# Mixing the first batch over its keys, scores two pairs ahead, and pooling by accumulating DMAs in a fused attention and MLP kernel

## The chip, the cores and the metric

The kernel runs on one core of one Trainium2 chip. A core has TensorE (PE, with its weight loads shown as PEld), VectorE (DVE), ScalarE (ACT), GpSimd (POOL) and SyncE (SP), each with its own queue of instructions that is worked through in order, and 16 DMA engines. The metric is the device time of one execution in microseconds (us), as the median of several executions. The profile is of one execution by the hardware profiler.

## The reference

Three stages follow one another. B = 8 batches, H = 8 heads, S = 576 positions, D = 64, so 512 channels.

```python
k_p = k.reshape(B, H, Sp, pool, D).mean(axis=3)      # pool = 8, Sp = 72 keys
v_p = v.reshape(B, H, Sp, pool, D).mean(axis=3)
attn = softmax(q @ k_p^T / 8)                        # rows over the 72 keys
x = attn @ v_p                                       # heads joined: B x 576 x 512
h = x^T @ U @ V                                      # mixing over positions, rank 32
u = x + h^T
x = u + relu(u @ w_ch1) @ w_ch2                      # first MLP, 512 -> 2048 -> 512
xn = layernorm(x) * g_ln
out = x + relu(xn @ w_ch1') @ w_ch2'                 # second MLP
```

`U` (576 x 32), `V` (32 x 576) and the weights arrive as 64-bit floats, and the kernel turns them into 32-bit ones itself.

## The kernel before, in words

Two heads make a pair, so a batch has four pairs and the kernel has 32 (the first pair has the number P = 0). For each pair the kernel loads q, k and v (`att_load`), adds the eight neighbours of each key and value (`att_prep`, `att_prep_v`: one reduction or a tree of additions, on DVE or POOL), makes five tiles of scores on PE (`att_s`), finds the extreme of each row and takes exponentials and the normalization (`att_m`: DVE, ACT, then DVE or POOL), turns the result so that keys lie on partitions (`att_t`), and multiplies by the values (`att_av`), which leaves x of the pair as `xT`. When the four pairs of a batch are done, x is turned back tile by tile (`att_xt`), split into a high and a low part, multiplied by U (`att_g`, `att_gs`) and by V (`att_vm`), and DVE adds the product to `xT`. That is u. The first MLP works on groups of 512 positions: `a_l1` makes a hidden block of 128 channels from four `hid` pairs (high and low part of u) and the weights `wh` and `wl`, `a_l2` multiplies it on. Eight hidden blocks stay resident, and the rest is done in later passes whose weights are decoded and stored meanwhile.

Every weight block must be decoded first: 64-bit words are loaded into `wraw` or `araw`, and five DVE instructions (the first may be ACT's) and a split into `wh` and `wl` follow. This goes on beside the attention.

Nothing is issued in the order in which it is written. Each operation is recorded with its possible engines, an assumed cost on each, and a priority: the sum of PE cost recorded before it, plus a bias. A list scheduler (`Order.schedule`) then gives every operation an engine and a place, and the buffers of a ring are handed out in the order of the program. What the program writes earlier therefore has priority, but an assumed cost decides the place. The instructions of an engine then run in that fixed order, whatever the real times are. Before, all DMAs but one small load are issued by SP.

In the steps of a batch, pair P's turning and multiplying are interleaved with the scores of pair P + 1:

```python
S_ = [s(N, t) for t in range(5)] if N < B * NP else [None] * 5   # N = P + 1
seq = [S_[0], R_[2], S_[1], T_[0], S_[2], S_[3], T_[1], S_[4], T_[2], R_[1], M_, V_[0]]
```

## Time and profile before

| | |
|---|---|
| median of 3 runs | 1776.09 us (1772.47 to 1776.58) |
| the profiled execution, its own time | 1774.35 us |
| its span (first to last instruction) | 1772.6 us |
| PE busy in the span | 1738.5 us (98%) |
| DVE, ACT, POOL busy | 973.2, 723.8, 745.9 us (55%, 41%, 42%) |

The profiled execution lies 1.7 us under the median, and 1.75 us of its time lie outside the span. A busy share is an average over the whole span; the stages differ much, and the rows below are taken by stage. The granted clock (PEclk) is a share of TensorE's full 2.4 GHz; its lower level is 1.2 GHz.

### The profile page before, as it was taken

The page shows a single profiled execution, that of the slowest core. Times are in us where ns is not written, and L with a number is a line of the kernel's source. Part 1 is how long each engine was busy: PE and PEld are TensorE (multiplying, and loading weights), DVE is VectorE, ACT ScalarE, POOL GpSimd, SP SyncE. Part 2 cuts the span into 40 slices and gives each one's busy share as a digit, 9 for nine tenths or more (in the row PEclk, how much of TensorE's full clock was granted, in tenths as well). Part 3 has the DMA queues.
Part 4 walks back from the last instruction along what each step waited for, and adds up shares of the span by engine and source line. Part 5 has one row for each costly group of instructions (what it writes and reads, how often), then busy time and mean ns, then how long its engine had stood idle before and what let it go on. Part 6 is the DMA issues. An engine that isn't in the chain of part 4 may idle for free.

```text
span 1772.6 us, 26907 instructions
## 1 busy us (share of the span) xinstructions
PE 1738.5 (98%) x10156; PEld 1519.6 (86%) x10156; DVE 973.2 (55%) x1858; ACT 723.8 (41%) x1897; POOL 745.9 (42%) x638
## 2 busy tenths in 40 slices
PE   5899999999999999999999999999999999999998
PEld 4678888888888889999999988999999999899997
DVE  8998888888646354444445766553224633333333
ACT  5556556655632233333333443333333433223221
POOL 1233224222100066666666653333334455555654
PEclk8799999999999999999999999999999999999999
DMA  6555544654343153544444444332112423233222
GB/s 194 179 165 181 189 162 155 206 182 132 108 141 112 42 196 123 123 120 122 121 120 106 132 130 157 119 122 81 48 48 84 143 101 102 102 114 112 102 78 78
DMA packets 95251, 222.97 MB, mean 126 GB/s; under 512 B 14225, under 2 KB 14225, under 8 KB 89361
## 3 DMA queue, kind: packets, MB, share of 16 engines
q1 hardware_dynamic: 94976, 221.25, 39.4%
q8 instruction: 79, 1.29, 0.3%
q14 instruction: 52, 0.42, 0.1%
q10 hardware_dynamic: 144, 0.00, 0.0%
HBM read 152.00 MB, written 69.22 MB: 125 GB/s over the span
## 4 chain that ended last, share of the span: by engine, by line
PE 94%; DVE 4%; DMA 1%; ACT 0%; issue 0%; DVEq 0%; ACTq 0%
PE py L1387 33%; PE pa L1299 17%; PE pbc L1299 13%; PE pbc L1097 11%; PE pa L1069 10%; PE py L378 3%; PE py L792 2%; PE py L918 1%; PE py L919 1%; PE py L900 1%; PE py L956 1%; PE py L957 0%; PE py L981 0%; PE pbc L1522 0%; DMA wraw<-w_d 0%
## 5 line engine op out<-in xcount | busy, mean ns | idle before, releaser
L1387 PE MATMUL py<-hid,w2h 128*128 128x512 f32 x1728 | 541.2, 394 | 0.2 <-DVE hid L1327 0.2
L1387 PE MATMUL py<-hid,w2l 128*128 128x512 f32 x864 | 338.6, 392 | 0.0
L1299 PE MATMUL pa<-op,w1h 128*128 128x256 f32 x1728 | 326.2, 281 | 0.5 <-ACT s L383 0.3
L1299 PEld LDWEIGHTS pa<-op,w1h 128*128 128x128 f32 x1728 | 293.9, 188 | 37.0 <-DVE s L385 0.6
L528 POOL TENSOR_TENSOR op<-xraw,op 128x512 fp32r<-128x512 f32 x130 | 171.5, 1321 | 280.2 <-ACT op L383 275.7
L1357 DVE TENSOR_TENSOR pbc<-s,pbc 128x512 f32<-128x512 f32 x108 | 75.1, 696 | 390.2 <-PE pbc L1299 386.0
L1387 PEld LDWEIGHTS py<-hid,w2h 128*128 128x128 f32 x1728 | 273.5, 189 | 11.0 <-DVE hid L1327 0.5
L1299 PEld LDWEIGHTS pbc<-op,w1h 128*128 128x128 f32 x1296 | 220.7, 188 | 28.1
L1299 PE MATMUL pbc<-op,w1h 128*128 128x256 f32 x1296 | 244.3, 281 | 0.0
L1299 PE MATMUL pa<-op,w1l 128*128 128x256 f32 x864 | 242.6, 281 | 0.0
L1387 PEld LDWEIGHTS py<-hid,w2l 128*128 128x128 f32 x864 | 162.4, 188 | 36.7
L1097 PE MATMUL pbc<-op,wh 128*128 128x512 f32 x576 | 183.7, 400 | 0.0
L1069 PE MATMUL pa<-hid,wh 128*128 128x512 f32 x576 | 181.9, 397 | 0.0
L1299 PE MATMUL pbc<-op,w1l 128*128 128x256 f32 x648 | 181.8, 280 | 0.0
L1299 PEld LDWEIGHTS pa<-op,w1l 128*128 128x128 f32 x864 | 162.9, 189 | 0.0
L1327 DVE SCALAR_TENSOR_TENSOR hid<-pa,hid 128x512 fp32r<-128x512 f32 x108 | 74.5, 690 | 123.8 <-ACT hid L1321 123.6
L1321 ACT ACTIVATE hid<-pa 128x512 fp32r<-128x512 f32 x108 | 64.6, 598 | 188.5 <-PE pa L1299 184.2
L1321 ACT ACTIVATE hid<-pbc 128x512 fp32r<-128x512 f32 x108 | 64.6, 598 | 184.9 <-DVE pbc L1357 183.9
L1253 POOL TENSOR_TENSOR t<-xraw 128x512 f32<-128x512 f32 x52 | 67.8, 1303 | 138.3 <-DMA xraw<-n_d 80.8
L1069 PEld LDWEIGHTS pa<-hid,wh 128*128 128x128 f32 x576 | 104.9, 188 | 20.9 <-issue 0.4
L1299 PEld LDWEIGHTS pbc<-op,w1l 128*128 128x128 f32 x648 | 121.9, 188 | 0.0
L1097 PEld LDWEIGHTS pbc<-op,wh 128*128 128x128 f32 x576 | 103.1, 188 | 20.8 <-issue 2.2
(187 smaller groups left out, 2896.0 us busy)
## 6 DMA issues: line engine op xcount, KB each, us to landing
xraw<-n_d SPq DMA_DIRECT2D x18, 1024.0 KB
wraw<-wC SPq DMA_DIRECT2D x32, 512.0 KB
wraw<-wA SPq DMA_DIRECT2D x24, 512.0 KB
w_d<-wx SPq DMA_DIRECT2D x48, 256.0 KB
wraw<-w_d SPq DMA_DIRECT2D x48, 256.0 KB
k<-kT SPq DMA_DIRECT2D x32, 288.0 KB
q<-qT SPq DMA_DIRECT2D x32, 288.0 KB
v<-v SPq DMA_DIRECT2D x32, 288.0 KB
```

What stands on the lines that cost most here:

```text
L378: e.matmul(out, src, ident, start=first, stop=True, is_transpose=True, skip_group_check=True)
L528: lambda e: e.tensor_sub(lo(), src(), hi().bitcast(F32)),
L792: lambda e: e.matmul(ps.t[:, i : i + 2 * SP], q.t[:, QT[t] : QT[t] + 128], kbd.t.rearrange("p h n -> p (h n)"), start=True, stop=True, ski ...
L900: lambda e: e.matmul(ps.t[:, :SH], vs.t[:, w], ef.t[:, h, c], start=(h == 0), stop=(h == 1)),
L1069: e.matmul(ps.t, w.t[:, c], u.t, start=(i == 0), stop=(i == 3 * NCC - 1))
L1097: e.matmul(ps.t, w.t[:, c], x.t, start=(f == 0 and j == 0), stop=(f == NA - 1 and j == 2))
L1253: o.op(on, lambda e: e.tensor_sub(dst(), a(), c()), r=r, w=w)
L1299: e.matmul(bank.t[:, sl], w.t[:, self.WCOL[k], c], u.t[:, t], start=(first and i == 0), stop=(last and i == 5), skip_group_check=True,)
L1321: lambda e: e.activation(h.t[:, :TG], bank.t, AF.Relu),
L1327: lambda e: e.scalar_tensor_tensor(l.t[:, :TG], bank.t, 0.0, h.t[:, :TG].bitcast(F32), op0=ALU.max, op1=ALU.subtract),
L1357: o.op({DVE: c_dve(TG)}, lambda e: e.tensor_add(c.t, s.t, c.t), r=[s], w=[c])
L1387: e.matmul(y.t, w.t[:, i, c], x.t[:, :TG], start=(first and q == 0), stop=(last and q == 2))
```

## The change

Four things change together.

- **The first batch is mixed over its keys.** x of a pair is attn times the pooled values, and mixing over positions acts on attn's positions alone. So for the four pairs of batch 0 the normalized scores `sc` (positions on partitions, 144 keys of the pair) are multiplied by U directly (`att_u`, five plain 32-bit products of 144 columns), the result is split as before into `gk`, and in `att_t` its product with V is added by PE onto the turned scores in the same PSUM buffer (one product of 512 columns for each of the two heads, two of 64 for the rest). What `att_av` then makes is already u. `att_xt`, `att_g`, `att_gs` and `att_vm` fall away for batch 0, and `att_out` splits and stores u pair by pair. U has a second, unsplit copy `us`, and its last block moves to the upper half of the partitions. Batches 1 to 7 are mixed as before.
- **Scores run two pairs ahead**: N = P + 2, and the rings `kbd`, `sc`, `mx`, `sm` and `vz` have three buffers instead of two, `vs` four instead of three. The scores of the first three pairs are put into the `pbc` buffers.
- **Keys and values of pairs 4 to 31 are pooled by DMAs that add.** SP loads one half of k, POOL issues a DMA that adds the other half onto it, and two more that fold the buffer onto itself (144 columns onto 144, 72 onto 72). The same for v. For pairs 0 to 3 both halves are loaded by SP into two buffers and added by an engine, then reduced as before. The host stores k so that the eight neighbours lie 72 columns apart.
- **The setup of U and V is recorded earlier**, right after the first pair's keys.

The diff, cut:

```diff
-UT = [0, 128, 256, 384, 512]
+UT = [0, 128, 256, 384, 448]
...
-        o.port = not any(b.ring.pool.space is PSUM for b in o.bufs)
+        o.port = not size and not any(b.ring.pool.space is PSUM for b in o.bufs)
...
-            if e == SY:
+            if o.size:
...
-        ring(att, "kbd", [128, 2, SP], n=2)
+        ring(att, "kbd", [128, 2, SP], n=3)
         ring(att, "q", [128, S], n=2)
-        ring(att, "k", [128, S])
-        ring(att, "v", [SP, 2, POOL * D])
+        ring(att, "k", [128, S // 2], n=2)
+        ring(att, "v", [SP, 2, POOL // 2 * D], n=2)
         ring(att, "kp", [128, SP], n=2)
-        ring(att, "vs", [SP, 4, D], F32R, 3)
-        ring(att, "vz", [SP, 3 * D], n=2)
+        ring(att, "vs", [SP, 4, D], F32R, 4)
+        ring(att, "vz", [SP, 3 * D], n=3)
...
-        ring(att, "sc", [128, 5, 2 * SP], n=2)
-        ring(att, "mx", [128, 10], n=2)
-        ring(att, "sm", [128, 10], n=2)
+        ring(att, "sc", [128, 5, 2 * SP], n=3)
+        ring(att, "mx", [128, 10], n=3)
+        ring(att, "sm", [128, 10], n=3)
...
+        ring(att, "us", [128, 5, 128])
+        ring(att, "gk", [128, 2 * SP], F32R, 2)
...
-                lambda e: e.memset(raw.t[64:, 4 * RANK : n].bitcast(I32), 0),
+                lambda e: e.memset(raw.t[:64, 4 * RANK : n].bitcast(I32), 0),
...
+        self.us = self.buf("us")
+        o.op({GP: 500}, lambda e: e.memset(self.us.t, 0.0), w=[self.us])
+        for c in (0, 1, 3):
...
+                lambda e, c=c: copy(nc, e, self.us.t[:, :, c * RANK : (c + 1) * RANK], u(x.t)),
...
+        two = P < DIRECT or P >= TREE
+        k = [self.buf("k") for _ in range(1 + two)]
+        v = [self.buf("v") for _ in range(1 + two)]
+        kd = lambda z: self.kT[b, p][:, z * (S // 2) : z * (S // 2) + S // 2]
...
+        vd = lambda z: self.v[b, 2 * p : 2 * p + 2].rearrange("h (k s) d -> k h (s d)", s=POOL)[:, :, z * n : z * n + n]
...
+        def load(x, of, z):
+            o.op({SY: 450}, lambda e: e.dma_start(x.t, of(z)), w=[x], size=147456)
+
+        def more(x, dst, src, n):
+            o.op({GP: C_SW}, lambda e: e.dma_start(dst(), src(), accum_op=ALU.add), w=[x], size=n)
+
+        load(k[0], kd, 0)
+        if two:
+            load(k[1], kd, 1)
         o.op({SY: 450}, lambda e: e.dma_start(q.t, self.qT[b, p]), w=[q], size=294912)
-        o.op(
-            {SY: 450},
-            lambda e: e.dma_start(v.t, self.v[b, 2 * p : 2 * p + 2].rearrange("h (k s) d -> k h (s d)", s=POOL)),
-            w=[v],
-            size=294912,
-        )
+        load(v[0], vd, 0)
+        if two:
+            load(v[1], vd, 1)
+        else:
+            K, V = k[0], v[0]
+            more(K, lambda: K.t, lambda: kd(1), 147456)
+            for z in (2, 1):
+                more(K, lambda z=z: K.t[:, : z * SP], lambda z=z: K.t[:, z * SP : 2 * z * SP], z * 36864)
+            more(V, lambda: V.t, lambda: vd(1), 147456)
+            for z in (2, 1):
+                more(V, lambda z=z: V.t[:, :, : z * D], lambda z=z: V.t[:, :, z * D : 2 * z * D], z * 36864)
...
-        kp, kbd = self.buf("kp"), self.buf("kbd")
...
-        o.op({DVE: c_dve(S), GP: c_pool(4 * SP) + c_pool(2 * SP) + c_pool(SP)}, pool, w=[k, kp])
+        kbd = self.buf("kbd")
+        if len(k) > 1:
+            k, rest = k
+            kp = self.buf("kp")
+            kv = lambda: k.t.rearrange("p (s n) -> p s n", n=SP)
+            o.op({DVE: c_dve(S // 2), GP: c_pool(S // 2)}, lambda e: e.tensor_add(k.t, k.t, rest.t), r=[rest], w=[k])
...
+            o.op({DVE: c_dve(S // 2), GP: c_pool(2 * SP) + c_pool(SP)}, pool, w=[k, kp])
+        else:
+            kp = k[0]
...
-                lambda e, r=r, h=h: scaled(nc, e, kbd.t[r, h], kp.t[r], -1.0 / (POOL * 8)),
+                lambda e, r=r, h=h: scaled(nc, e, kbd.t[r, h], kp.t[r, :SP], -1.0 / (POOL * 8)),
...
+        if rest:
+            z = rest[0]
+            o.op({GP: c_pool(2 * n), DVE: c_dve(2 * n)}, lambda e: e.tensor_add(v.t, v.t, z.t), r=[z], w=[v])
...
+        elif P < LEAN_T:
+            on = {ACT: c_act(2 * D), DVE: c_fast(2 * D), GP: c_pool(2 * D)}
+            o.op(on, lambda e: copy(nc, e, lean(), v.t[:, :, :D]), r=[v], w=[vs])
...
-            self.sps[P, t // 3] = self.buf("py")
+            self.sps[P, t // 3] = self.buf("pbc" if P < EARLY else "py")
...
+        if P < NP:
+            gs = self.gk[P]
+            whole = (j, slice(0, 512), slice(0, 512))
+            parts = [whole] if j < 2 else [(h, slice(h * 64, h * 64 + 64), slice(512, S)) for h in range(2)]
+
+            def add(e):
+                for h, a, k in parts:
+                    e.matmul(
+                        ps.t[:SP, a], gs.t[:, h * SP : h * SP + SP], self.vst.t[:, k], start=False, stop=True,
+                        skip_group_check=True,
+                    )
+
+            o.op({PE: 320 if j < 2 else 2 * 107}, add, r=[gs, self.vst], w=[ps])
...
-                turn(e, ps.t[:n, p * 128 : p * 128 + 128], xs[p].t[:, UT[i] : UT[i] + n], self.ident, p == 0)
+                turn(e, ps.t[:, p * 128 : p * 128 + 128], xs[p].t[:, UT[i] : UT[i] + 128], self.ident, p == 0)
...
-            if b == 0:
-                self.a_split(0, c, View(x, None, lambda t: t[:, :TG]))
...
+    def att_u(self, P):
+        nc, o = self.nc, self.o
+        sc, ps = self.sc[P], self.buf("py")
+        n = 2 * SP
+
+        def mm(e):
+            for t in range(5):
+                e.matmul(ps.t[:, :n], self.us.t[:, t], sc.t[:, t], start=(t == 0), stop=(t == 4))
+
+        o.op({PE: 5 * 240}, mm, r=[sc, self.us], w=[ps])
...
+        o.op({ACT: c_act(n, True)}, lambda e: copy(nc, e, gr.t, ps.t[:, :n]), r=[ps], w=[gr])
+        o.op(
+            {DVE: c_dve(n) + 60},
+            lambda e: e.scalar_tensor_tensor(
+                gs.t, gr.t.bitcast(F32), self.neg_b, ps.t[:, :n], op0=ALU.mult, op1=ALU.add
...
+        self.gk[P] = gs
+
+    def att_out(self, P):
+        o = self.o
+        x = self.xT[P]
+        self.a_split(0, P, View(x, None, lambda t: t[:, :TG]))
+        self.ud[0, P] = d = Buf(None)
+        o.op({SY: 450}, lambda e: e.dma_start(self.u_d[:, P, :S], x.t), r=[x], w=[d], size=294912)
...
-        first = [ld(0), pr(0), pv(0), ld(1)] + [s(0, t) for t in range(5)] + [pr(1), pv(1), ld(2)]
-        first += [m(0)]
-        for P in range(B * NP):
-            N = P + 1
-            last = P % NP == NP - 1
-            S_ = [s(N, t) for t in range(5)] if N < B * NP else [None] * 5
-            M_ = m(N) if N < B * NP else None
-            R_ = [ld(P + 3), pr(P + 2), pv(P + 2)] if P + 2 < B * NP else [None] * 3
+        U = lambda P: [lambda: self.att_u(P)] if P < NP else []
+        S = lambda P: [s(P, t) for t in range(5)]
+        n = B * NP
+        first = [ld(0), pr(0), self.setup_uv, pv(0), ld(1), *S(0), pr(1), pv(1), ld(2), m(0), *S(1), m(1)]
+        first += [pr(2), pv(2), ld(3), *U(0)]
+        for P in range(n):
+            N = P + 2
+            b, last = P // NP, P % NP == NP - 1 and P >= NP
+            S_ = S(N) if N < n else [None] * 5
+            M_ = m(N) if N < n else None
+            R_ = [ld(P + 4), pr(P + 3), pv(P + 3)] if P + 3 < n else [None] * 3
...
             if not last:
                 seq = [S_[0], R_[2], S_[1], T_[0], S_[2], S_[3], T_[1], S_[4], T_[2], R_[1], M_, V_[0]]
                 seq += [V_[1], R_[0], V_[2], V_[3]]
+                seq += ([lambda P=P: self.att_out(P)] if P < NP else []) + U(P + 1)
             else:
...
-        self.setup_uv_at = len(per[0]) // 2
-        for i, st in enumerate(per[0]):
-            if i == self.setup_uv_at:
-                self.setup_uv()
+        for st in per[0]:
...
+C_SW = 950.0
+DIRECT = 4
+TREE = B * NP
+EARLY = 3
...
+    def spread(x):
+        return np.ascontiguousarray(pairs(x).reshape(B, NP, 2 * D, SP, POOL).transpose(0, 1, 2, 4, 3)).reshape(B, NP, 2 * D, S)
```

How this moves the instructions is shown at three places, as they stand on an engine's queue. The numbers in the names are those of buffers; they differ between the two programs.

PE before, from the last products of batch 0's mixing to the first MLP product (L981 is the product with V, L792 makes scores from the keys `kbd`, L378 turns, L1069 is the MLP):

```order
L981 MATMUL py_246<-vstk_189,gs_187 128x288
L981 MATMUL py_247<-vstk_189,gs_187 128x288
L792 MATMUL py_249<-kbd_154,q_156 128x144 x2
L378 MATMUL py_248<-ident,sc_167 72x128 x4
L792 MATMUL py_249<-kbd_154,q_156 128x144
L792 MATMUL py_246<-kbd_154,q_156 128x144
L378 MATMUL py_247<-ident,sc_167 72x128 x4
L792 MATMUL py_246<-kbd_154,q_156 128x144
L378 MATMUL py_248<-ident,sc_167 72x64 x2
L1069 MATMUL pa_242<-hid_209,wh_220 128x512
```

PE of the change, the same place (L925 adds the product of `gk` and V, L956 multiplies by the values, L835 makes scores, L1154 is the MLP):

```order
L378 MATMUL py_257<-ident,sc_172 72x64 x2
L925 MATMUL py_257<-vstk_200,gk_199 72x64 x2
L956 MATMUL py_259<-ef_171,vz_168 128x288 x2
L956 MATMUL py_260<-ef_171,vz_168 128x288 x2
L835 MATMUL py_257<-kbd_153,q_156 128x144 x2
L378 MATMUL py_259<-ident,sc_173 72x128 x4
L835 MATMUL py_257<-kbd_153,q_156 128x144
L835 MATMUL py_258<-kbd_153,q_156 128x144
L378 MATMUL py_260<-ident,sc_173 72x128 x4
L835 MATMUL py_258<-kbd_153,q_156 128x144
L378 MATMUL py_259<-ident,sc_173 72x64 x2
L1154 MATMUL pa_253<-hid_220,wh_231 128x512
```

Before, the scores just ahead of the first MLP product are those of pair 5, and the turned scores those of pair 4. Now the scores are those of pair 6, whose keys come from the second set of adding DMAs into `k_158`, and the turned scores are still those of pair 4.

POOL before, at the corresponding place (L772 and L746 add values and keys, L528 makes low parts):

```order
L772 TENSOR_TENSOR v_158<-v_158 72x2x128
L528 TENSOR_TENSOR wl_227<-ax_151,wh_226 128x512
L772 TENSOR_TENSOR v_158<-v_158 72x2x256
L746 TENSOR_TENSOR k_157<-k_157 128x72x4
L746 TENSOR_TENSOR k_157<-k_157 128x72x2
L747 TENSOR_TENSOR kp_160<-k_157 128x72
L528 TENSOR_TENSOR hid_210<-xT_177,hid_209 128x512
```

POOL of the change, from the keys of pair 4 (`k_158`) and pair 5 (`k_159`) on; after these rows two more value additions stand, then the same for pairs 6 and 7:

```order
L747 DMA k_158<-k_158 128x144
L747 DMA k_159<-k_159 128x144
L747 DMA v_160<-v 72x2x256
L530 TENSOR_TENSOR wl_232<-wx_145,wh_231 128x512
L747 DMA k_158<-k_158 128x72
L747 DMA v_161<-v 72x2x256
L747 DMA k_159<-k_159 128x72
L747 DMA v_160<-v_160 72x2x128
L747 DMA v_161<-v_161 72x2x128
L747 DMA v_160<-v_160 72x2x64
L747 DMA v_161<-v_161 72x2x64
L747 DMA k_158<-kT 128x288
```

The additions have left POOL's and DVE's lists, and twelve DMAs for two pairs stand in POOL's, each waiting for an earlier one of its buffer; a low part of a weight stands among them.

SP of the change, where the weight loads (L696) now stand behind key loads that wait for POOL's DMAs:

```order
L696 DMA araw_150<-wA 128x512
L744 DMA k_158<-kT 128x288
L744 DMA k_159<-kT 128x288
L696 DMA wraw_144<-wA 128x512
L752 DMA q_156<-qT 128x576
L744 DMA v_160<-v 72x2x256
L696 DMA araw_150<-wA 128x512
```

These key loads are for pairs 6 and 7 and need the buffers that pairs 4 and 5 fill; before, key loads stood ahead of weight loads in the same way and waited for DVE's or POOL's reduction.

## Rows read from the trace of the kernel before

**Rows 1.** Windows by stage: us, busy (x instructions) by engine, PEclk, DMA share, GB/s

```profile
0.00:69.57 69.57, 45.61 (x175) 34.41 (x176) 57.83 (x137) 37.74 (x145) 13.28 (x29) 0.77 0.61 196
...
13.15:71.76 58.61, 45.05 (x175) 33.70 (x176) 52.46 (x119) 33.12 (x122) 11.52 (x11) 0.71 0.56 183
71.76:92.82 21.06, 18.21 (x96) 14.60 (x95) 20.72 (x45) 13.91 (x66) 5.85 (x7) 1.00 0.47 146
92.82:150.40 57.58, 57.58 (x298) 47.23 (x297) 50.50 (x113) 35.38 (x128) 16.93 (x17) 1.00 0.60 193
150.40:620.00 469.60, 468.79 (x2388) 389.32 (x2387) 336.39 (x694) 237.76 (x787) 97.86 (x112) 1.00 0.44 143
```

**Rows 2.** What PE waited for, 0 to 135 us: us, times, longest

```profile
PE py L378 <- DVE sc L842: 6.9, 4, 2.9
...
PE py L981 <- DVE gs L967: 3.5, 1, 3.5
```

**Rows 3.** PE timeline: start, length, instruction; the first MLP product and what precedes it

```profile
67.23 1.29 PE L792 MATMUL py<-kbd,q 128*128 128x144 f32 x4
...
71.76 0.73 PE L1069 MATMUL pa<-hid,wh 128*128 128x512 f32 x2
```

**Rows 4.** Chain that ended last, pieces with start and length: the spacing of PE instructions

```profile
95.92 1.46 PE py L900 x6
97.38 0.74 PE py L792 x6
...
107.39 0.87 PE py L378 x8
...
114.20 0.23 PE py L956
...
126.17 0.52 PE py L981 x4
```

**Rows 5.** DVE by line and form, 0 to 135 us: count, busy, mean ns

```profile
L842 DVE TENSOR_TENSOR sc<-sc,sm 128x720 f32<-128x720 f32 x9 | 8.7, 969 | 0.1
L772 DVE TENSOR_TENSOR v<-v 72x512 f32<-72x512 f32 x11 | 8.5, 773 | 2.6 <-DMA v<-v 2.6
L743 DVE TENSOR_REDUCE kp<-k 128x72 f32<-128x576 f32 x9 | 6.6, 737 | 3.6 <-DMA k<-kT 3.6
L988 DVE TENSOR_TENSOR xT<-xT,py 128x288 f32<-128x288 f32 x16 | 6.2, 447 | 0.7 <-PE py L981 0.7
...
L528 DVE TENSOR_TENSOR wl<-wx,wh 128x512 fp32r<-128x512 f32 x7 | 4.8, 684 | 0.1
```

**Rows 6.** DVE timeline: the last split of u for the first MLP group

```profile
68.18 1.39 DVE L528 TENSOR_TENSOR hid<-xT,hid 128x512 fp32r<-128x512 f32 x1
```

**Rows 7.** DMA landings in the chain that ended last: start, us to landing

```profile
0.74 2.86 DMA k<-kT
...
24.18 2.90 DMA q<-qT
...
80.79 5.24 DMA v<-v
```

**Rows 8.** SP's issue of key loads, 0 to 130 us: issue time ns min/median/max

```profile
L725 SPq DMA_DIRECT2D k<-kT x14: 327/328/458, 0.7 to 105.9; - x14
```

**Rows 9.** POOL by line and form, 0 to 135 us

```profile
L528 POOL TENSOR_TENSOR hid<-xT,hid 128x512 fp32r<-128x512 f32 x3 | 4.2, 1446 | 17.1 <-DVE hid L385 17.1
L528 POOL TENSOR_TENSOR wl<-ax,wh 128x512 fp32r<-128x512 f32 x3 | 3.9, 1306 | 19.5 <-DVE wh L385 10.7 <-ACT wh L383 8.8
```

**Rows 10.** Chain that ended last: first MLP product of the second and third group

```profile
150.40 2.73 PE pa L1069 x12
...
216.51 2.94 PE pa L1069 x12
```

More of the change, by code (lines that the diff above doesn't have):

```diff
@@ L628, in load @@
             )
-            o.op({SY: 450}, lambda e: e.dma_start(raw.t[:64, 4 * RANK : n], self.U[512:]), w=[(raw, 1)], size=16384)
+            o.op({SY: 450}, lambda e: e.dma_start(raw.t[64:, 4 * RANK : n], self.U[512:]), w=[(raw, 1)], size=16384)
         x = self.staged(n, load)
@@ L634, in u @@
             return t[:, :n].rearrange("p (i r) -> p i r", r=RANK)
+        self.us = self.buf("us")
+        o.op({GP: 500}, lambda e: e.memset(self.us.t, 0.0), w=[self.us])
+        for c in (0, 1, 3):
+            o.op(
+                {ACT: c_act(n), DVE: c_fast(n)},
+                lambda e, c=c: copy(nc, e, self.us.t[:, :, c * RANK : (c + 1) * RANK], u(x.t)),
+                r=[x],
+                w=[(self.us, c)],
+            )
         for c in (0, 1, 3):
@@ L661, in load @@
                     )
-            x = self.staged(SH, load)
+            x = self.staged(SH, load, 'aw'[z])
             o.op(
@@ L760, in att_prep_v @@
     def att_prep_v(self, P):
-        o = self.o
-        v = self.raw[P][2]
+        nc, o = self.nc, self.o
+        v, rest = self.raw[P][2][0], self.raw[P][2][1:]
         vs = self.vs[P] = self.buf("vz" if P < LEAN_T else "vs")
-        n = POOL * D
-        while n > D:
-            n //= 2
-            to, w = (lambda n=n: v.t[:, :, :n]), [v]
-            if P < LEAN_T and n == D:
-                to, w = (lambda: vs.t.rearrange("p (a d) -> p a d", d=D)[:, 0:3:2]), [v, vs]
-            o.op(
-                {GP: c_pool(2 * n), DVE: c_dve(2 * n)},
-                lambda e, n=n, to=to: e.tensor_add(to(), v.t[:, :, :n], v.t[:, :, n : 2 * n]),
-                w=w,
-            )
+        n = POOL // 2 * D
+        lean = lambda: vs.t.rearrange("p (a d) -> p a d", d=D)[:, 0:3:2]
+        if rest:
+            z = rest[0]
+            o.op({GP: c_pool(2 * n), DVE: c_dve(2 * n)}, lambda e: e.tensor_add(v.t, v.t, z.t), r=[z], w=[v])
+            while n > D:
+                n //= 2
+                to, w = (lambda n=n: v.t[:, :, :n]), [v]
+                if P < LEAN_T and n == D:
+                    to, w = lean, [v, vs]
+                o.op(
+                    {GP: c_pool(2 * n), DVE: c_dve(2 * n)},
+                    lambda e, n=n, to=to: e.tensor_add(to(), v.t[:, :, :n], v.t[:, :, n : 2 * n]),
+                    w=w,
+                )
+        elif P < LEAN_T:
+            on = {ACT: c_act(2 * D), DVE: c_fast(2 * D), GP: c_pool(2 * D)}
+            o.op(on, lambda e: copy(nc, e, lean(), v.t[:, :, :D]), r=[v], w=[vs])
         if P < LEAN_T:
@@ L874, in att_t @@
         o.op({PE: cost}, mm, r=[sc], w=[ps])
+        if P < NP:
[7 more added lines that the diff above has]
+                        skip_group_check=True,
+                    )
+            o.op({PE: 320 if j < 2 else 2 * 107}, add, r=[gs, self.vst], w=[ps])
         if P < LEAN_T:
@@ L938, in mm @@
             for p in range(NP):
-                turn(e, ps.t[:n, p * 128 : p * 128 + 128], xs[p].t[:, UT[i] : UT[i] + n], self.ident, p == 0)
+                turn(e, ps.t[:, p * 128 : p * 128 + 128], xs[p].t[:, UT[i] : UT[i] + 128], self.ident, p == 0)
         o.op({PE: 4 * 110}, mm, r=xs, w=[ps])
-        top = lambda t: t[:n]
+        whole = lambda t: t
         if NP * b < LEAN_X:
-            self.split_ps(View(xh, None, top), View(xl, None, top), ps, top, DM, n)
+            self.split_ps(View(xh, None, whole), View(xl, None, whole), ps, whole, DM, 128)
         else:
-            self.split(View(xh, None, top), View(xl, None, top), View(ps, None, top), DM, ps=True, hi_on=(ACT,))
-        self.xhl[i] = (xh, xl, n)
+            self.split(View(xh, None, whole), View(xl, None, whole), View(ps, None, whole), DM, ps=True, hi_on=(ACT,))
+        self.xhl[i] = (xh, xl)
     def att_g(self, b, i):
@@ L952, in att_g @@
         pg = self.pg
-        xh, xl, n = self.xhl[i]
+        xh, xl = self.xhl[i]
         def mm(e):
-            e.matmul(pg.t, self.ust.t[:n, i], xh.t[:n], start=(i == 0), stop=False)
-            e.matmul(pg.t, self.ust.t[:n, i], xl.t[:n], start=False, stop=(i == 4))
+            e.matmul(pg.t, self.ust.t[:, i], xh.t, start=(i == 0), stop=False)
+            e.matmul(pg.t, self.ust.t[:, i], xl.t, start=False, stop=(i == 4))
         self.o.op({PE: c_pe(DM, 2)}, mm, r=[xh, xl, self.ust], w=[pg])
@@ L1123, in phase_a @@
         o = self.o
[L1124 removed]
+        self.raw, self.qk, self.vs, self.sc, self.et, self.sps, self.xps, self.gk = {}, {}, {}, {}, {}, {}, {}, {}
         self.xT, self.xhl, self.ut, self.hid, self.wres = {}, {}, {}, {}, {}
@@ L1647 @@
         "qT": pairs(q),
-        "kT": pairs(k),
+        "kT": spread(k),
         "v": np.ascontiguousarray(v),
```

28 lines of the change are left out of this document (15 added, 13 removed).

## The prediction

> **What bounds the kernel now.** I read the windows by stage first. From 92.8 us to 150.4 PE is busy without a gap at full clock, and from there to 620 us it is idle for 0.8 us [rows 1]. What can be won or lost therefore lies in three places: the start, PE's own work, and new waits in a stretch that has none. In the start, from 13.15 to 71.76 us, PE is busy for 45.05 of 58.61 us, so 13.6 are idle, and the granted clock is 0.71 of full, which is the lower level of 1.2 GHz for more than half of the time [rows 1]. The list of waits says for whom: the normalized scores of DVE (6.9 us in 4 waits) and the split product of batch 0's mixing (3.5 us) [rows 2]. DVE is the bound there. It is busy for 57.83 of the first 69.57 us with 137 instructions [rows 1], and that stretch ends with the last split of u for the first group of the MLP [rows 6]. PE works off the scores and turns that stand ahead in its queue and begins the MLP at 71.76 us [rows 3]. From there to 92.82 us it loses another 2.85 us [rows 1], since weights are still being decoded. After that it is never free.
>
> **DVE up to the first MLP product.** I count the instructions that stand in DVE's queue up to that last split and give each the mean of its form, of which [rows 5] shows the larger ones. Before, the 137 instructions make 64.8 us; they overlap a little and wait a little, and the end came at 69.57, so 4.8 us behind the sum. In the change 134 instructions stand there. Gone are the 8 additions of the mixed product (0.447 each, 3.6 us). The keys fall from 7.4 to 4.6 us: a reduction took 0.737, and now an addition of half length and a reduction of half length do it for four pairs, which I price at 0.45 each by the addition of 288 columns (between nothing saved and a half; the other pairs need none on DVE). The values fall from 8.0 to 4.9 us, since POOL's DMAs fold pairs 4 and 5. Added are one more pair's softmax (2.4 us, 0.969 of it the normalization), three splits that were POOL's (0.68 each) and four small splits of `gk` at 0.3 in place of one of 0.74. The decoding stays (29.1 to 28.6 us). The sum is 60.8 us, and 4.8 behind it is 65.6. With the same 2 us on PE behind it, as before, the MLP begins at 67.5 us, 4.3 earlier.
>
> **PE's work.** The spacing at full clock is 0.123 us for an instruction of a score product (two to a product), 0.243 for one of a value product, 0.109 for a turn, 0.23 for a product of 512 columns and 0.13 for one of 288 [rows 4]. Batch 0 loses 20 turns, 15 products of 512 and 8 of 288: 6.7 us. It gains 20 products with U, priced as score products because they have their columns and number format (4.9 us), 8 of 512 (1.8) and 8 of 64 columns, at most a turn each (0.9): 7.6 us. So 1.0 us of work is added, not removed. The last tile of U with 128 instead of 64 positions changes the other operand's width only and costs nothing that I count. Ahead of the first MLP product PE had 27.3 us of such work and now has 29.5; of the difference 1.2 is five score products that would come later anyway, because scores run two pairs ahead.
>
> **After the first MLP product.** By the time of the last split, DVE has passed the weights of six of the eight hidden blocks. Each block is 2.73 us of PE [rows 10], so PE holds over 16 us of work and DVE has to make only two blocks more. Of the 2.85 us lost here I leave 1.0.
>
> **The sum.** 4.3 us earlier, 1.2 us of scores already done, 1.85 less waiting: 7.3 us. The profiled execution took 1774.35 us, so 1767; it lay 1.7 under the median, against which I forecast 1769 us. Nothing is won later: PE is full there, and what DVE and POOL save goes into idle time.
>
> **What hides the new DMAs.** Twelve adding DMAs serve two pairs, on POOL's queue, in order. No row shows such a DMA. The nearest are SP's loads: they land after 2.86 or 2.90 us in the start and 5.24 at worst [rows 7], and SP spends 0.33 us on an issue [rows 8]. From below I take 0.33, as if the issue were all, from above 5.24; I use 2.9, since these are of half a load's size or less and start in the same stage, and 0.33 for POOL's issue, with a whole landing as its upper end. Of the queue, pair 6 matters first: its scores stand ahead of the first MLP product on PE. Its chain begins behind `wl_232` on POOL, which waits for DVE's cast of that weight. DVE's sum to there is 35.5, plus 4.8 is 40.3; the subtraction takes 1.31 [rows 9]: 41.6 us. Behind it stand five landings one after another (two value steps of pair 5, then three key steps of pair 6) and a dozen issues: 14.5 + 4, so 60.1 us. The keys' scaling, scores and turns are 5 us more [rows 3]: 65, under the 67.5 that DVE needs. They are hidden by 2.5 us. ACT scales keys in the same queue as exponentials, and SP's weight loads stand behind key loads, so if this chain is late, decoding and exponentials are late too.
>
> A rule of the Trainium skill speaks against this step. POOL and DVE disturb each other already: while POOL split three tiles at 1.45 us each [rows 9], DVE's split took 1.39 us [rows 6] where the form takes 0.68 [rows 5]. The Trainium skill, page "SBUF — State Buffer", section "SBUF: two separate sides", says that descriptors of a DMA from GpSimd are written by its cores and cannot be written while VectorE runs an operation in a mode that takes the shared ports. If each adding DMA is delayed by what that DVE row lost, 0.7 us, a landing is 3.6, the chain of pair 6 ends at 68.5, and 1 us of the 7.3 is lost. On the other side the page "DMA: Bandwidth & Descriptors", section "Anatomy of one DMA — SWDGE (gpsimd) path", gives about 2.0 us plus bytes over 436 GB/s, an estimate of 2.3 for the largest here; by it the chain would be hidden by more.
>
> **Rivals.** *PE stays slow in the start (no change).* Per pair, four steps in series are new on PE, ACT and DVE before a result can be turned, and PE takes its queue in order. Before, 26.1 us of work after the first pair's scores took 58.61 us, 2.25 times as long, through gaps and the lower clock [rows 1]. If the new 27 us stretch alike from 14.5 us on (DVE's sum to the first normalization is 10.9, behind 3.6 for the first keys), the MLP begins at 75.2 us, 3.4 later, less 1.2 and 1.85: nothing: 1774 for the profiled execution, 1776 for the median. For it: PE's clock was at its lower level even where it was busy. Against: with scores two pairs ahead there is more to do in a gap.
>
> *POOL's queue is too slow (slower).* Two pairs take 33.05 us of a batch's 66.1 [rows 10]. The twelve DMAs are six landings deep, with 4 us of issues and some 3 of other POOL work: 24.4 us at 2.9, 38.4 at 5.24. Beyond 4.3 us for a landing PE waits for keys in every pair. At 5.24 it is 5.4 us for each of twelve double pairs, 65 us, and about 1840. For it: POOL's issue may hold the queue longer than SP's, and waiting DMAs stop what stands behind. Against: the data are smaller than a load that lands in 2.9.
>
> *DVE's gaps close (more gained).* Of the first 69.57 us DVE was idle for 11.7 [rows 1], 3.6 of it for the first keys [rows 5]. With pairs further ahead the rest may go; then the keys of pair 6 bind at 65 us, and with no wait left the time is 3.5 us lower: about 1765.
>
> **Chances.** The forecast, 1769 with 1764 to 1773 of its own: 0.46. PE slow, 1776: 0.25. POOL too slow: 0.18. DVE's gaps close: 0.11. The range reaches over all but most of POOL's case: 1762 to 1783. A change under 0.3% (5.3 us) is about what a measurement cannot tell from none. Faster by more: nearly all of the forecast and all of the fourth, 0.53; slower by more, most of POOL's case: 0.17; between them 0.30.
>
> **What would show it.** The first MLP product (L1154) at 65 to 70 us, with DVE at work up to it; 74 or later with PE's clock at 0.7 is the first rival. A landing of POOL's DMAs near 2.9, and no PE wait for `kbd` after 100 us; waits of L835 for keys, or of POOL for its own DMAs of over 4.3 us, are the second. What would make the forecast wrong is a POOL issue that costs microseconds, or weights that arrive late at SP behind key loads.

## The result, and the profile after

The changed kernel takes 1788.7 us (median of four, 1785.83 to 1791.58); the kernel before, beside it, 1776.34. The ratio is 1.0076, 95% interval 1.0062 to 1.0091: 12 us slower, where 7 us faster was forecast. The profiled execution took 1791.26 us, with a span of 1789.2.

The windows of [rows 1], now of the changed kernel:

```profile
0.00:69.57 69.57, 44.99 (x206) 37.27 (x206) 55.97 (x138) 32.90 (x155) 31.98 (x50) 0.85 0.82 201
...
71.76:92.82 21.06, 20.57 (x108) 17.08 (x107) 17.04 (x37) 13.55 (x58) 13.89 (x14) 1.00 0.88 202
92.82:150.40 57.58, 53.81 (x277) 42.98 (x277) 47.82 (x105) 34.50 (x132) 36.38 (x34) 1.00 0.92 215
150.40:620.00 469.60, 458.83 (x2306) 379.56 (x2305) 317.54 (x671) 220.72 (x746) 147.02 (x143) 0.99 0.56 148
```

Read the first pair of numbers behind the length, PE. From 92.82 to 620 us, where it had been idle for 0.8 us, it now misses 3.77 + 10.77 us, 13.7 more. The two profiled spans lie 16.6 us apart (1772.6 and 1789.2), a little more than the medians. In the first stretch PE still misses as much as before. The fifth pair is POOL: from 13.28 to 31.98 us in the first stretch, from 97.86 to 147.02 in the last. The last column but one is the DMA engines' share: from 92.82 to 150.40 us 0.92, where it was 0.60.

PE's timeline at the first MLP product (in brackets, the idle time ahead):

```profile
70.63 0.30 PE L378 MATMUL py<-ident,sc 64*72 64x64 f32 x2 [1.83 <-ACT ef L383]
70.86 0.73 PE L1154 MATMUL pa<-hid,wh 128*128 128x512 f32 x2
```

It stands at 70.86 us; the forecast was 67.5, before it was 71.76 [rows 3]. What held it back, by the timelines of PE, DVE and ACT:

```profile
44.04 1.33 PE L835 MATMUL py<-kbd,q 128*128 128x144 f32 x4 [5.34 <-ACT kbd L390]
...
65.06 0.76 PE L835 MATMUL py<-kbd,q 128*128 128x144 f32 x4 [1.57 <-ACT kbd L390]
```

```profile
65.78 0.68 DVE L530 TENSOR_TENSOR hid<-xT,hid 128x512 fp32r<-128x512 f32 x1
```

```profile
69.44 0.53 ACT L390 ACTIVATE kbd<-k 64x72 f32<-64x72 f32 x2 [4.43 <-DMA k<-k]
```

The keys `kbd` of pairs 4 to 7 are scaled by ACT out of a `k` that the adding DMAs have folded. PE waits 5.34 us for those of pair 4 and 1.57 for those of pair 6. DVE is done with its last split of u for the first MLP group at 66.46 us. But ACT stands 4.43 us, until 69.44, for the folded keys of pair 7; the copy `ef` is behind them in its queue, and for it waits the turn that stands ahead of the MLP product (the 1.83 us above). So the product comes 4.4 us behind the split, where it came 2.2 behind it before [rows 3, 6]. Some landings of adding DMAs in the start, from the chain of 10 to 71 us that ended last, which is that of POOL's queue (start, us to landing):

```profile
28.90 5.08 DMA k<-kT
...
35.75 6.63 DMA v<-v
...
60.59 5.00 DMA v<-v
```

Now the adding DMAs, of which before had none. First the DMA queues in 20 to 500 us (packets, MB, share of 16 engines) and the issues (KB each, median us to landing):

```profile
q1 hardware_dynamic: 34558, 68.92, 46.0%
q0 software_dynamic: 29568, 14.49, 24.9%
...
k<-kT POOLq DMA_DIRECT2D x28, 144.0 KB, 5.0
v<-v POOLq DMA_DIRECT2D x28, 144.0 KB, 4.6
...
k<-k POOLq DMA_DIRECT2D x28, 72.0 KB, 4.3
v<-v POOLq DMA_DIRECT2D x28, 72.0 KB, 4.1
k<-k POOLq DMA_DIRECT2D x28, 36.0 KB, 4.4
v<-v POOLq DMA_DIRECT2D x28, 36.0 KB, 4.7
```

Then the same DMAs among POOL's groups (count, busy us, mean ns, idle before):

```profile
L747 POOL DMA_DIRECT2D v<-v x84 | 105.1, 1300 | 65.1 <-DMA v<-v 49.5 <-DMA k<-kT 6.4 <-ACT sc L867 3.0
...
L747 POOL DMA_DIRECT2D k<-k x56 | 60.8, 1106 | 47.9 <-DMA k<-k 25.1 <-DMA k<-kT 18.8 <-DVE sm L881 2.4
...
L747 POOL DMA_DIRECT2D k<-kT x28 | 32.5, 1229 | 6.6 <-DMA k<-kT 5.9 <-issue 0.6
```

One keeps POOL for 1.1 to 1.3 us, SP's issue takes 0.33 [rows 8]; it lands after 4.1 to 5.0 us, whatever its size from 36 to 144 KB; and a MB on this queue costs the DMA engines 2.6 times what one on SP's does (24.9/14.49 against 46.0/68.92). After 92.82 us PE waits mostly for DVE, in the mixing of the batches:

```profile
PE py L1036 <- DVE gs L1022: 3.2, 2, 2.6
PE py L1012 <- DVE xl L530: 2.8, 3, 1.7
PE py L1036 <- DVE xT L1043: 2.1, 2, 1.4
```

And what DVE waits for, from 92.82 to 620 us, first in the changed kernel, then before:

```profile
DVE wt L570 <- DMA wraw<-wA: 17.1, 6, 5.1
DVE wt L570 <- DMA wraw<-wC: 16.8, 8, 3.8
...
DVE vs L385 <- DMA v<-v: 6.8, 2, 3.5
```

```profile
DVE wt L568 <- DMA wraw<-wC: 5.6, 3, 4.5
...
DVE wt L568 <- DMA wraw<-wA: 2.1, 3, 1.0
```

It waits for raw weights and values. PE waits for no key (`kbd`) after 100 us.

### The profile page after: what moved, and what is told of

The parts are those of the page before. It is cut to its first block, busy times and chain, and to the rows that moved or that the text cites. A ratio compares the mean times of both kernels' runs of the same rounds, so it can differ in the third digit from the quotient of the medians.

```text
span 1789.2 us, 27142 instructions
## 1 busy us (share of the span) xinstructions
PE 1740.5 (97%) x10169; PEld 1522.9 (85%) x10169; DVE 949.8 (53%) x1830; ACT 707.7 (40%) x1877; POOL 840.2 (47%) x716
## 3 DMA queue, kind: packets, MB, share of 16 engines
q0 software_dynamic: 29568, 14.49, 6.7%
## 4 chain that ended last, share of the span: by engine, by line
PE 80%; DMA 10%; DVE 6%; issue 2%; POOL 1%; ACT 1%; SPq 0%; DVEq 0%; POOLq 0%; ACTq 0%
PE py L1469 33%; PE pa L1381 17%; PE pbc L1381 12%; PE pbc L1182 9%; PE pa L1154 5%; DMA wraw<-wA 3%; DMA v<-v 3%; DMA k<-k 2%; DMA wraw<-wC 1%; PE py L378 1%; PE py L835 1%; DMA k<-kT 1%; DVE wx L595 1%; DVE wx L587 1%; DMA wraw<-w_d 1%
## 5 line engine op out<-in xcount | busy, mean ns | idle before, releaser
L1154 PE MATMUL pa<-hid,wh 128*128 128x512 f32 x576 | 181.9, 397 | 1.5 <-DVE op L1161 1.5
L747 POOL DMA_DIRECT2D v<-v x84 | 105.1, 1300 | 65.1 <-DMA v<-v 49.5
L1335 POOL TENSOR_TENSOR t<-xraw 128x512 f32<-128x512 f32 x52 | 67.2, 1293 | 137.7 <-DMA xraw<-n_d 80.4
L1154 PEld LDWEIGHTS pa<-hid,wh 128*128 128x128 f32 x576 | 105.3, 188 | 22.5 <-DVE op L1161 1.9
```

The source lines that it names most:

```text
L747: o.op({GP: C_SW}, lambda e: e.dma_start(dst(), src(), accum_op=ALU.add), w=[x], size=n)
L1154: e.matmul(ps.t, w.t[:, c], u.t, start=(i == 0), stop=(i == 3 * NCC - 1))
L1335: o.op(on, lambda e: e.tensor_sub(dst(), a(), c()), r=r, w=w)
```

## The experiments

The theory that this profile suggests: the adding DMAs cost more than the pooling they replace (A), either through order and lateness (A1) or through time that they take from the DMA engines (A2) or from GpSimd, which the profile calls POOL (G). The rival: mixing over the keys, or two pairs ahead, costs it (B). Unless said otherwise an edit is made to the changed kernel; the edits are shown cut. Each kernel gets its whole order anew from the planner, and that alone may move the time: a second tile for raw weights, with nothing else changed, moved it by +1.7, +6 and +8 us (e17, e15, e14 below). No difference of that size is laid to a cause by its size alone.

**Without the adding DMAs.**

```diff
-TREE = B * NP
+TREE = 4
```

> The changed kernel without any adding DMA (TREE = 4): all 32 pairs are loaded in two halves by SP and pooled by the engines; batch 0 mixed over the keys and scores two pairs ahead stay. Theory A (the adding DMAs themselves make the 12 us: their time on the DMA engines, or their slow landing): the loss goes, 1772 to 1777 us, with TensorE idle in 92 to 400 us below 2 us. Theory B (mixing batch 0 over the keys, or running two pairs ahead, costs it): it stays at 1785 to 1789 us.

1779.2 us, ratio 1.0028 (1.0017 to 1.0039). It is 9.5 us under the changed kernel, and PE's loss after 150.40 us goes with it, from 10.77 to 0.97 us: A. It is still 4 us over the kernel before that ran beside it (1774.9), and these 4 us have a place in the windows of e1:

```profile
0.00:69.57 69.57, 47.75 (x236) 38.35 (x236) 59.23 (x147) 38.02 (x178) 18.83 (x37) 0.88 0.67 192
...
71.76:92.82 21.06, 21.00 (x113) 17.32 (x111) 20.74 (x46) 14.99 (x62) 3.48 (x5) 1.00 0.57 171
92.82:150.40 57.58, 49.09 (x227) 39.43 (x228) 55.71 (x117) 28.54 (x95) 23.06 (x20) 0.94 0.63 193
150.40:620.00 469.60, 468.63 (x2387) 391.38 (x2386) 339.21 (x700) 230.84 (x761) 84.87 (x99) 1.00 0.44 142
```

Up to 92.82 us PE misses 5 us less than in [rows 1]; then it misses 8.5 us up to 150.40, with DVE busy for 55.71 of 57.58. The start was won and given back in the next stage, where all of PE's waits are for DVE. POOL's groups of e1 in 100 to 400 us tell what pooling costs there:

```profile
L804 POOL TENSOR_TENSOR v<-v,v 72x512 f32<-72x512 f32 x17 | 26.2, 1541 | 39.2 <-DMA v<-v 33.9 <-DMA k<-kT 4.3 <-DVE wt L580 0.9
...
L774 POOL TENSOR_TENSOR k<-k,k 128x288 f32<-128x288 f32 x14 | 13.3, 947 | 16.1 <-DMA k<-kT 16.1
L812 POOL TENSOR_TENSOR v<-v 72x256 f32<-72x256 f32 x12 | 11.1, 929 | 3.2 <-DVE v L804 2.5
L812 POOL TENSOR_TENSOR v<-v 72x128 f32<-72x128 f32 x13 | 7.5, 578 | 4.6 <-DVE v L812 3.8
...
L780 POOL TENSOR_TENSOR k<-k 128x144 f32<-128x144 f32 x9 | 5.6, 617 | 0.9 <-DVE k L774 0.8
...
L781 POOL TENSOR_TENSOR kp<-k 128x72 f32<-128x72 f32 x9 | 3.7, 415 | 21.2 <-ACT kbd L390 18.3 <-DVE sm L881 2.0 <-DVE kbd L392 0.4
```

Done wholly on POOL, a pair's pooling is the sum of the six means, 5.0 us. Its six adding DMAs keep POOL for 198.4 us over 28 pairs, 7.1 us a pair. The DMAs take more of POOL than the work they take off it; what they save is DVE's part of it.

**The two other parts.** e9 is e1 with batch 0 mixed over its channels as before, e13 is e1 with scores one pair ahead.

```diff
-        if P < NP:
+        if P < KEYS:
...
+KEYS = 0
```

> e1_no_adding with batch 0 mixed over its channels as before: of the change only scores two pairs ahead, the halved loads and the earlier U and V stay. If mixing over the keys brings the earlier start (first MLP product 69.7 in e1_no_adding, 71.8 before) and two pairs ahead cost the 4 us: 1780 to 1785 us. If mixing over the keys is the cost: 1773 to 1777 us.

```diff
-            N = P + 2
+            N = P + 1
...
-            R_ = [ld(P + 4), pr(P + 3), pv(P + 3)] if P + 3 < n else [None] * 3
+            R_ = [ld(P + 3), pr(P + 2), pv(P + 2)] if P + 2 < n else [None] * 3
```

> e1_no_adding with the scores one pair ahead instead of two: of the change mixing batch 0 over the keys, the halved loads and the earlier U and V. If mixing over the keys alone costs the 4 to 6 us between e9_ahead_alone and e1_no_adding: 1778 to 1784 us. If only the two together do (more work before the first product than VectorE can carry): 1772 to 1776 us.

e9: 1773.1 us, ratio 0.9989 (0.9979 to 1.0000). e13: 1777.2, 1.0014 (1.0000 to 1.0028). e9 lies where mixing over the keys was to be the cost, e13 between its two ranges. The differences are no larger than those of the second tile, so what part of the 4 us is rival B's stays open. The first MLP product stood at 75.0 us in e9, 73.7 in e13, 69.7 in e1, and the kernel with the latest one was the fastest: its place alone does not tell the time.

**Lateness (A1).** e2 lets the planner reckon with the measured issue and landing; e14 gives raw weights a second tile; e15 and e17 do so without adding DMAs.

```diff
-C_SW = 950.0
+C_SW = 1100.0
+SW_MORE = 2000.0
...
-                o.end = dma + 1000
+                o.end = dma + 1000 + (SW_MORE if e == GP else 0.0)
```

> The changed kernel with the same adding DMAs, but the planner that fixes the order reckons with what the trace showed: 1100 ns of GpSimd for an issue and a landing 2 us later. Theory A1 (the loss is order: keys, values and the SP queue behind them come later than planned): most of it goes, 1774 to 1780 us. Theory A2 (the loss is time of the DMA engines that the many small read-add-write packets take from the weight loads): the same DMAs run, so it stays at 1785 to 1790 us.

```diff
-        ring(stg, "wraw", [128, 512], I64)
+        ring(stg, "wraw", [128, 512], I64, n=2)
```

> The changed kernel with a second tile for raw weights (wraw 2 instead of 1), so that a weight load is issued one weight earlier; the 168 adding DMAs are unchanged. In 90 to 450 us VectorE stood 34 us until weights landed, against 12 us before. Theory A2 in its stronger form (the adding DMAs hurt because they make the weights late): most of the 12 us go, 1776 to 1782 us. If VectorE's waits only move to the next thing that is late (values, keys, GpSimd): 1785 to 1792 us.

> e9_ahead_alone (two pairs ahead alone, no adding DMA) with the second tile for raw weights. VectorE waited 24 us for weights in 90 to 620 us there, while TensorE was idle for under 2 us in 92 to 620: hidden. If so, no change, 1770 to 1775 us; if the waits set the decoding of the resident weights before 92 us, 1766 to 1770 us.

> The kernel before with the second tile for raw weights, as the control of the two others: 1771 to 1777 us if it is of no use there.

e2: 1799.2 us. e14: 1797.0. Neither cure helps. In e14 DVE's waits for raw weights are gone from the head of its list, but PE still misses 9.0 us in 150 to 400 us, and POOL now waits 83 us for its own DMAs on `v` in 90 to 450. The chain that ended last, followed back from 400 to 150 us, holds landings of raw weights for 27% of its time in the changed kernel (none before); in e14 it holds landings of the adding DMAs on `k` and `v` for 33%. The late weights were where the cost showed, not all that made it. So e2 and e14 do not clear lateness: take one late thing away, and the next stands in the chain. The controls: e15 1779.3 (6 over e9), e17 1777.0.

**Dose.** e4 adds only the second half by DMA (2 a pair, 56 in all) and folds on the engines; e6 has adding DMAs for batch 1 alone, e7 for batches 2 to 7 alone, and e12 is e9 with those of batch 1.

```diff
-            for z in (2, 1):
-                more(K, lambda z=z: K.t[:, : z * SP], lambda z=z: K.t[:, z * SP : 2 * z * SP], z * 36864)
```

> Only the second half from HBM is added by a DMA (2 a pair instead of 6, 8.26 of the 14.45 MB); the folds to one half and one quarter go back to the engines. Theory A1 (the chain of three landings behind each other is late): one landing of 4 to 5 us instead of three, so two thirds of the loss go, 1776 to 1781 us. Theory A2 (engine time by bytes): about four tenths of it go, 1781 to 1785 us. If it is by the number of DMAs (GpSimd's issues), two thirds go under A2 too.

```diff
-TREE = B * NP
+TREE = 8
```

> Adding DMAs for the four pairs of batch 1 alone (TREE = 8; 24 of 168); pairs 8 to 31 in halves by SP, pooled by the engines. In e1_no_adding VectorE was busy 56 of the 58 us of 92 to 150 us and TensorE lost 8.6 us there; in the changed kernel the loss of 92 to 150 us was 3.8, and 10.7 more came in 150 to 400 us. If relief of VectorE at batch 1 is worth having and the later adding DMAs do the harm: the loss of 92 to 150 falls to 4 to 5 us and that after 150 goes, 1772 to 1776 us. If adding DMAs in the start cost as much as they relieve: 1778 to 1782 us.

```diff
-DIRECT = 4
+DIRECT = 8
```

> The complement: adding DMAs for pairs 8 to 31 (DIRECT = 8; 144 of 168), batch 1 pooled by the engines. If the harm is done after 150 us by the adding DMAs of batches 2 to 7: the loss of 92 to 150 us as in e1_no_adding (8 us) and 8 to 11 us in 150 to 400, 1786 to 1792 us. If the harm is the adding DMAs in the start, beside the 16 weight loads of the first stage: 1776 to 1781 us.

> e9_ahead_alone (two pairs ahead, batch 0 over its channels) with adding DMAs for the four pairs of batch 1 alone, which took 3 us off e1_no_adding. If they relieve VectorE here too: 1768 to 1772 us, below both kernels. If the relief was only of what mixing over the keys had pushed into 92 to 150 us: 1773 to 1777 us.

e4: 1788.3, no gain, though two thirds of the DMAs are gone. By its windows it loses half as much as the changed kernel after 150.40 us (5.6 of 10.8), and 7.4 from 92.82 to 150.40, nearly what e1 loses there, with DVE busy for 54.6 of the 57.6. e6: 1776.0, ratio 1.0009 (0.9999 to 1.0020). e7: 1796.2, so the adding DMAs of batches 2 to 7 cost 17 us over e1; added to e6 they make the changed kernel, 12.7 over it. e12: 1782.4, 9 us over e9, against the 3 us that the same DMAs gave e1: its start suffers (PE busy for 18.5 of the first 45 us, 26.95 in e9; the MLP begins at 85.6). That relief at batch 1 is worth having is therefore not shown.

**Idle adding DMAs.** On top of e1, into scratch: e5 as in the changed kernel, each waiting for the one before; e8 spread over four tiles; e11 as e8 without the addition; e10 fills by POOL in place of DMAs.

```diff
+            sk, sv = self.buf("sk"), self.buf("sv")
+            more(sk, lambda: sk.t, lambda: kd(1), 147456)
```

> The kernel of e1_no_adding, in which the engines pool, with the 168 adding DMAs put on top, into scratch tiles that nobody reads; plain loads and pooling by the engines stay, so the traffic is larger than in the changed kernel (14.45 MB more). Theory A1 (only waiting for their landings costs): as e1_no_adding within 3 us. Theory A2 (their time on the DMA engines, or GpSimd's issues): 1785 us or more.

```diff
+            idle(0, lambda t: t, lambda: kd(1), 147456)
+            idle(1, lambda t: two(t[:SP]), lambda: vd(1), 147456)
```

> As e5_idle_adding (e1_no_adding with 168 idle adding DMAs of the same sizes on top), but spread over four scratch tiles and fixed sources, so that GpSimd hardly ever waits for an earlier one to land. Theory W (GpSimd, in order, stands at each adding DMA until the one before has landed, and its other work with it): most of the 50 us of e5 go, 1783 to 1795 us remain. Theory A2 (the DMA engines' time): still 1815 us or more, since the packets are the same.

```diff
-                o.op({GP: C_SW}, lambda e: e.dma_start(dst(x[i].t), src(), accum_op=ALU.add), r=r, w=[x[i]], size=n)
+                o.op({GP: C_SW}, lambda e: e.dma_start(dst(x[i].t), src()), r=r, w=[x[i]], size=n)
```

> e8_idle_no_wait with the same 168 idle transfers from GpSimd, but plain, without the addition. If the addition makes them costly for the DMA engines: the queue's time falls to less than half of e8's 22.9% of 20 to 500 us, and the time to 1785 to 1797 us. If it is that GpSimd issues them (theory G): 1805 us or more, as e8.

```diff
+            def fill(e):
+                e.memset(busy.t, 0.0)
+                e.memset(busy.t, 0.0)
+
+            for _ in range(6):
+                o.op({GP: C_SW}, fill, w=[busy])
```

> e1_no_adding (engines pool, no adding DMA) with 168 pieces of idle GpSimd work of 1.2 us each, two fills of a scratch tile, put where e8_idle_no_wait had its adding DMAs (an adding DMA keeps GpSimd busy for 1.1 to 1.3 us by the rows of the changed kernel). No DMA is added. Theory G (it is GpSimd's time that the issues take, and VectorE's, which takes over GpSimd's work): most of the 35 us of e8_idle_no_wait show, 1800 us or more. Theory A2 (the DMA engines' time): 1779 to 1788 us.

Over e1: e5 +50 (1829.3), e8 +35 (1813.9), e10 +14 (1793.5), e11 +10 (1789.1). e8's time lies above the 1795 that theory W allowed and just under the 1815 of A2; e10 lies between its two theories; e11 fits the addition. The queue of e8 in 20 to 500 us, then that of e11:

```profile
q0 software_dynamic: 22944, 14.18, 22.9%
```

```profile
q0 software_dynamic: 7016, 14.09, 10.2%
```

The same bytes in a third of the packets and under half of the engines' time, when nothing is added. POOL too is held for less, by the largest of its groups in e8 and in e11:

```profile
L773 POOL DMA_DIRECT2D jk<-us x111 | 114.5, 1208 | 67.2 <-DMA jk<-v 36.8 <-DMA jk<-kT 21.5 <-DMA jk<-us 5.6
```

```profile
L773 POOL DMA_DIRECT2D jk<-us x109 | 61.6, 567 | 52.3 <-DMA jk<-v 21.6 <-DMA jk<-kT 19.2 <-DMA jk<-us 10.1
```

So the addition itself is dear: by the medians 25 of the 35 us, though e8's runs lie 18 us apart (1804.7 to 1823.1). In e8 POOL still waits for its own DMAs (67.2 us ahead of this group alone), so the waiting was not taken away.

**Free pooling.** The pooling of pairs 4 to 31 is left out.

```diff
-            more(K, lambda: K.t, lambda: kd(1), 147456)
...
+            k2, v2 = self.buf("k"), self.buf("v")
+            load(k2, kd, 1)
+            load(v2, vd, 1)
```

> The changed kernel with the pooling of pairs 4 to 31 left out: both halves are loaded by SP as in e1_no_adding, nothing is added, and the first eighth stands for the pooled keys and values. It is what adding DMAs would give if they cost nothing, neither GpSimd nor the DMA engines. If the idea was worth 7 us or more and only its carrier is dear: 1762 to 1770 us. If VectorE's share of pooling was no bound: 1772 to 1778 us.

1755.95 us, ratio 0.9892 (0.9879 to 0.9906), 6 us better than the best expected. Its windows, and the instructions of its first MLP product's line up to 80 us (duration ns, first and last start us):

```profile
0.00:69.57 69.57, 51.71 (x261) 41.99 (x262) 60.75 (x161) 43.68 (x204) 12.21 (x31) 0.93 0.77 222
13.15:71.76 58.61, 51.13 (x268) 41.44 (x269) 55.81 (x147) 39.49 (x184) 10.60 (x11) 0.91 0.77 228
71.76:92.82 21.06, 21.06 (x106) 17.44 (x105) 19.83 (x45) 15.51 (x62) 1.71 (x2) 1.00 0.73 212
92.82:150.40 57.58, 57.58 (x311) 48.51 (x310) 49.66 (x109) 37.21 (x130) 9.12 (x9) 1.00 0.58 185
```

```profile
L1150 PE MATMUL pa<-hid,wh x22: 387/394/504, 64.1 to 79.9; 128*128 128x512 f32 x22
```

PE starts the MLP at 64.1 us, is full from 71.76 to 150.40, and is granted 0.91 of its clock from 13.15 to 71.76 us, where it was 0.71 [rows 1]. The idea is worth 19 us if its carrier is free. Against e16, pooling on the engines costs 23 us (e1) and pooling by adding DMAs 33 (the changed kernel).

**The 33 us taken apart.** e18 is e16 with e10's fills; e19 is the changed kernel with its adding DMAs aimed at e8's scratch tiles, so that its pooling is left out too.

```diff
+            for _ in range(6):
+                o.op({GP: C_SW}, fill, w=[busy])
```

> e16_free_pooling (pooling of pairs 4 to 31 left out, 1756 us) with the 168 idle pieces of GpSimd work of e10_pool_busy, 1.2 us each. It takes GpSimd's time alone, with no load on the DMA engines and nothing that lands late. Between e16_free_pooling and the changed kernel lie 33 us. If GpSimd's time for the issues is most of them: 1778 us or more. If it is the DMAs: 1757 to 1767 us (GpSimd had only 20 of 150 us to do in 250 to 400 there).

```diff
-            more(K, lambda: K.t, lambda: kd(1), 147456)
...
+            idle(0, lambda t: t, lambda: kd(1), 147456)
```

> The changed kernel with its adding DMAs aimed at scratch tiles that nobody reads: same loads by SP, same number, sizes and queue of adding DMAs as the changed kernel, pooling left out (the first eighth stands for the pooled keys and values). Nobody waits for a landing but, now and then, a later adding DMA into the same scratch tile. If waiting for landings is the cost: 1760 to 1768 us. If the DMA engines' time and GpSimd's are: 1780 to 1789 us. What lies between this and e18_free_pool_busy is the DMA engines', what lies between this and the changed kernel the waiting.

e18: 1782.3 us (1781.2 to 1788.3). e19: 1778.6 (1774.0 to 1792.4). By medians the fills cost 26 us over e16, the adding DMAs that nobody reads 23, and the changed kernel lies 10 above these. They are not shares of one sum, as e18 is above e19, and the traces say why. First the windows of e18, then those of e19:

```profile
0.00:69.57 69.57, 43.30 (x222) 35.59 (x222) 53.28 (x128) 40.35 (x197) 42.52 (x80) 0.93 0.65 190
...
92.82:150.40 57.58, 49.11 (x230) 38.84 (x230) 54.67 (x101) 33.63 (x107) 30.85 (x40) 0.91 0.57 178
150.40:620.00 469.60, 469.60 (x2387) 392.38 (x2385) 328.08 (x672) 232.26 (x765) 168.38 (x251) 1.00 0.45 145
```

```profile
0.00:69.57 69.57, 49.44 (x230) 40.59 (x231) 57.31 (x146) 39.55 (x184) 41.41 (x63) 0.86 0.95 230
...
92.82:150.40 57.58, 52.53 (x270) 43.58 (x269) 48.08 (x106) 30.52 (x113) 39.81 (x43) 0.97 0.86 204
150.40:620.00 469.60, 461.89 (x2333) 383.43 (x2333) 329.39 (x685) 219.37 (x719) 108.79 (x116) 1.00 0.53 147
```

Two rows tell how far the two stand for the changed kernel, the fills of e18 up to 80 us (duration ns, first and last start us) and a group of POOL's in e19:

```profile
L765 POOL MEMSET busy<- x36: 592/597/823, 3.1 to 80.0; 128x600 f32 x36
```

```profile
L765 POOL DMA_DIRECT2D jk<-us x112 | 109.9, 1142 | 85.5 <-DMA jk<-v 41.8 <-DMA jk<-us 19.4 <-DMA jk<-kT 12.9
```

The fills stand on POOL's queue from 3.1 us on, and e19's adding DMAs from 4.3, where the changed kernel has its first at 28.90. So both load the start earlier than the changed kernel does, and the first MLP product comes at 81.2 us in e18 and at 70.6 in e19. And POOL waits for landings of its own DMAs in e19 as long as in the changed kernel (111 and 106 us over all groups). What e19 takes away is the waiting of the engines for keys and values, and of SP for their buffers; 10 us is about what the second tile moved, and e19's runs lie 18 us apart.

With POOL busy, PE is idle for 26.3 us in the first stretch and 8.5 in the third (e16: 17.9 and none), and never after, though POOL is busy for 168 us there. Idle adding DMAs lose 7.7 us after 150.40, of the changed kernel's 10.8. So the later loss comes with the DMAs, not with POOL's time alone, and mostly without the engines' waiting for keys and values. Whether it is the time of the DMA engines or POOL's standing for landings, no run separates. In the start POOL's time and the DMAs' can both do harm; in the changed kernel the waits for landings shown above are part of it, and the rest is left open.

## Why the prediction was wrong

*The step that failed* is "What hides the new DMAs", with its conclusion "They are hidden by 2.5 us" and its term of 2.9 us for a landing. By the medians a landing took 4.1 to 5.0 us, and those shown of the start 5.00 to 6.63. They were not hidden: PE waited 5.34 us for the keys of pair 4, and its last turn ahead of the MLP stood behind the keys of pair 7, which the working left out.

The larger part failed with the sentence "Nothing is won later: PE is full there". The working let the adding DMAs cost something only up to pair 6 or, in a rival, through keys; the stretch after 92.82 us was put at nothing, and 13.7 us were lost in it. The adding DMAs are a load on three shared things there: POOL is held 1.1 to 1.3 us by each (0.33 was used), the engines work 2.6 times as long per MB, and waiting DMAs stop POOL. PE's later idle time goes through DVE, and not because DVE has more to do: from 150.40 to 620 us it is busy for 317.54 us, before for 336.39 [rows 1], and stands waiting instead. The last sentence of the prediction named both signs, an issue that costs microseconds and weights that arrive late; the sum had the first at 0.33 us and the second not at all.

*DVE's sum up to the first split* held: the split ended at 66.46 us, forecast 65.6 (the terms that are listed make 59.7, not the 60.8 that was used). *The MLP's start* did not: it came 0.9 us earlier instead of 4.3, since not DVE but ACT's keys were the last thing ahead of it. With the pooling on the engines (e1) it stands at 69.7, with none at 64.1: less load there does bring it forward, by more than forecast, but pooling holds it back by either carrier.

*PE's work*: 1.0 us was forecast; the busy sum rose from 1738.5 to 1740.5. *The loss in 71.76 to 92.82*: 1.0 forecast, 0.49 measured; right, and of no use.

*The landing* was put at 2.9 us and measured 4.1 to 5.0. The estimate of 2.3 from the Trainium skill (page "DMA: Bandwidth & Descriptors", section "Anatomy of one DMA — SWDGE (gpsimd) path") is half of the 4.6 and 5.0 us at 144 KB; the trace does not agree. The 3.6 us that were worked out for a delay by VectorE were nearer and still low. The rule behind them is the Trainium skill's, page "SBUF — State Buffer", section "SBUF: two separate sides"; no run here shows whether such a delay is part of the landings.

*The rivals.* "POOL's queue is too slow" named the right part, and landings did reach the 4.3 us that it set, but its price was another: PE was to wait for keys in every pair, 65 us. PE waits for the keys of adding DMAs ahead of the MLP and for none after 100 us; the later loss comes through DVE, and the whole of it is a fifth of that price. "PE stays slow in the start" does not show its sign, as the MLP began before 74 us. "DVE's gaps close" is nearest to e16, where DVE is idle for 8.8 us of the first 69.57 (11.7 before), but e16 also has less to do.
